# The last ten result tiles of a convolution-and-MLP kernel, stored one by one instead of in pairs

## Chip, cores, metric

One core of a Trainium2 chip. The metric is device microseconds of one execution. The kernel before takes 695.6 us (median of 3 runs, 695.6 to 696.04).

## The reference, cut to what matters

```python
# attention part: causal convolution, 7 taps, softmaxed per-head weights, x is (8, 4096, 192)
out = np.einsum('hk,bskhg->bshg', w, x_unf)
# then, on the 32768 rows:
h = x @ w_in                 # 192 -> 2048
g = np.maximum(0.01 * h, h)
return (g @ w_out)           # 2048 -> 192, float32
```

## The kernel before

The output is 256 tiles ("sums") of 128 rows by 192 columns. TensorE accumulates each in a PSUM bank, an engine copies it to SBUF, and SyncE's queue stores it. Two neighbouring sums share one SBUF buffer and go out in one store of 192 KB:

```python
o_pool = ctx.enter_context(tc.tile_pool(name="o", bufs=4))
...
NSUB = len(subs)             # 256
LAST = NSUB - 2 * SUB        # 248: the sums of the last block
...
def evac_o(n):
    b, e, s = subs[n]
    rp, st = divmod(b, NB)
    if n % 2 == 0:
        osb[n // 2] = o_pool.tile([128, 2, D], FP32, name="o_sb")
    o_sb = osb[n // 2]
    copy = nc.scalar.copy if b < NHALF else nc.vector.tensor_copy
    ins = copy(out=o_sb[:, n % 2, :], in_=po.pop(n))
    if n % 2 == 1:
        t0 = st * ST + (s - 1) * 128
        nc.sync.dma_start(
            out=out_rows[2 * rp + e, t0 : t0 + 256, :].rearrange("(c p) d -> p c d", p=128),
            in_=osb.pop(n // 2),
        )
    return ins
...
evac_o(LAST - 1)
for n in range(LAST, NSUB):            # nothing but these matmuls is left here
    po[n] = psum_o.tile([128, D], FP32, name="po", tag="po")
    for fc in range(NFC):
        mm2_one(None, n, fc, fc == 0, fc == NFC - 1)
    evac_o(n)
```

## Time and profile before

| part of the span | us | what it is |
|---|---|---|
| start to 689.91 | 689.9 | TensorE busy, 99% |
| to 690.31 | 0.4 | VectorE copies the last sum |
| to 692.33 | 2.0 | the last store: issue, packets, confirmation |
| to 692.68 | 0.35 | closing waits of SyncE, after the landing |
| to 693.5 | 0.8 | drains and barrier of all engines |

The span in the trace is 693.5 us; the measured time of that execution is 695.24 us, so 1.7 us lie around it. A store has "landed" when its semaphore, a counter that finished transfers raise, has its full value. The "closing waits" are the end of the program on SyncE: it waits for nine semaphores, one after the other. The rows come from the timeline and from windows cut at its times. The prediction below shows those lines. "The tail" in what follows is the last three rows: from the end of the last copy to the end of the span. Read with the page's rounding it is 693.5 - 690.31 = 3.19 us; the instruction records themselves give 3.235.

The page's list of transfers has the stores as one group, 128 of 192 KB, with the median time from issue to landing as its last column:

```profile
out_dram<-o_sb SPq DMA_DIRECT2D x128, 192.0 KB, 2.1
```

### The profile page before, as it was taken

Reading aid. Unit: us, or ns where it says so; the run is one execution under the profiler, and the core shown is the slowest. Engines: PE = TensorE matmul, PEld = TensorE weight load, DVE = VectorE, ACT = ScalarE, POOL = GpSimd, SP = SyncE. Lnnn points to the kernel's source line nnn. Section 1 sums busy time; section 2 is a strip of 40 time slices with the busy share of each in tenths; the row PEclk is TensorE's granted clock in tenths of the full one; section 3 lists DMA queues with packets and bytes.
Section 4 is the critical chain, followed back from the end, with each engine's and each line's share of the span. In section 5 each row is a group of like instructions: output and inputs, shape, how many; then the busy total and the mean of one; then the engine's idle time right before and its main releaser. Section 6 shows DMA issues by size and latency. Waiting matters only on the chain.

```text
span 693.5 us, 26049 instructions
## 1 busy us (share of the span) xinstructions
PE 683.7 (99%) x11778; PEld 539.4 (78%) x11778; DVE 543.9 (78%) x1005; ACT 516.4 (74%) x577; POOL 139.7 (20%) x195
## 2 busy tenths in 40 slices
PE   7999999999999999999999999999999999999997
PEld 5899998677777777777777777777777777777777
DVE  7899998977878787878787878877878878777812
ACT  6788888977777777777777777777777777777771
POOL 3632201502222202222112222102222022000000
PEclk9999999999999999999999999999999999999999
DMA  9995535935566345565355564545655365222112
GB/s 169 122 103 81 88 66 79 92 75 74 67 93 81 68 82 69 73 87 82 68 80 77 75 82 82 77 67 80 80 82 81 70 82 68 62 60 62 45 36 70
DMA packets 184015, 54.39 MB, mean 78 GB/s; under 512 B 148320, under 2 KB 183136, under 8 KB 183904
## 3 DMA queue, kind: packets, MB, share of 16 engines
q0 software_dynamic: 97936, 14.17, 30.3%
q1 hardware_dynamic: 85968, 38.56, 22.4%
q8 instruction: 92, 1.51, 1.0%
q14 instruction: 19, 0.16, 0.1%
HBM read 29.88 MB, written 25.17 MB: 79 GB/s over the span
## 4 chain that ended last, share of the span: by engine, by line
PE 93%; DMA 3%; DVE 2%; ACT 1%; POOL 0%; issue 0%; SPq 0%; POOLq 0%; DVEq 0%
PE po L391 48%; PE ph L365 45%; DVE yt L180 2%; DMA w_in<-in_moe_w_in_dram 1%; DMA x_nat<-in_x_dram 1%; DMA xt<-x_bf 1%; ACT g L372 0%; POOL sel L226 0%; DVE yt L174 0%; ACT x_bf L126 0%; POOL w_in L236 0%; PE ptr L141 0%; DVE x_bf L126 0%; SPq L441 0%; POOL sel L224 0%
## 5 line engine op out<-in xcount | busy, mean ns | idle before, releaser
L372 ACT ACTIVATE g<-ph 128x1024 bf16<-128x1024 f32 x512 | 496.2, 1021 | 156.2 <-PE ph L365 155.8
L180 DVE SCALAR_TENSOR_TENSOR yt<-xt,wk,yt 128x512 bf16<-128x512 bf16 (+1 forms) x648 | 442.3, 683 | 17.6
L391 PEld LDWEIGHTS <-g 64*128 64x128 bf16 (+1 forms) x8064 | 352.2, 94 | 45.3 <-issue 0.2
L391 PE MATMUL po<-w_out,g 64*128 64x192 bf16 (+1 forms) x8064 | 382.7, 243 | 0.0
L365 PE MATMUL ph<-yt,w_in 64*128 64x512 bf16 (+1 forms) x3552 | 379.3, 347 | 2.7 <-DMA w_in<-in_moe_w_in_dram 1.1
L365 PEld LDWEIGHTS <-w_in 64*128 64x128 bf16 x3552 | 186.5, 94 | 98.1 <-issue 4.6
L77 POOL DMA_DIRECT2D x_bf<-in_x_dram x180 | 133.7, 774 | 422.1 <-DMA xt<-x_bf 419.7
L438 DVE COPY o_sb<-po 128x192 f32<-128x192 f32 x216 | 77.1, 357 | 121.5 <-PE po L391 115.5
L174 DVE TENSOR_SCALAR yt<-xt,wk 128x512 bf16<-128x512 bf16 (+1 forms) x108 | 37.5, 347 | 2.0 <-DMA xt<-x_bf 1.9
L438 ACT COPY o_sb<-po 128x192 f32<-128x192 f32 x40 | 12.8, 320 | 1.9
L248 PE MATMUL warm<-zero 128*128 128x256 bf16 x24 | 4.8, 348 | 1.1 <-DVE junk L216 1.1
L199 PE MATMUL acc<-xt,diag 64*64 64x256 bf16 x84 | 5.2, 270 | 0.5 <-DVE xt L155 0.5
L199 PEld LDWEIGHTS <-diag 64*64 64x64 bf16 x84 | 4.3, 106 | 1.2 <-DVE xt L155 0.8
L303 ACT ACTIVATE diag<-ident,whm 128x64 bf16<-128x64 bf16 x14 | 3.5, 335 | 1.9 <-DVE whm L289 1.9
L248 PEld LDWEIGHTS <-zero 128*128 128x128 bf16 x24 | 2.4, 118 | 2.1 <-DVE junk L216 1.1
L494 POOL COPY pjunk<-g 1x1 bf16<-1x1 bf16 x1 | 0.2, 176 | 16.0 <-ACT g L372 16.0
L126 DVE CAST x_bf<-x_nat 128x384 bf16<-128x384 f32 x5 | 2.3, 454 | 1.4 <-DMA x_nat<-in_x_dram 1.4
L141 PE MATMUL ptr<-ident,x_bf 64*128 64x64 bf16 x48 | 1.4, 191 | 1.8 <-ACT x_bf L126 0.9
L141 PEld LDWEIGHTS <-x_bf 64*128 64x128 bf16 x48 | 1.0, 95 | 2.8 <-ACT x_bf L126 2.2
L236 POOL DMA_DIRECT2D w_in<-in_moe_w_in_dram x4 | 2.6, 660 | 0.0
L155 DVE COPY xt<-ptr 128x384 bf16<-128x384 bf16 x7 | 2.2, 351 | 0.5 <-PE ptr L141 0.4
L253 ACT ACT_TABLE_LOAD x1 | 1.3, 1283 | 0.8 <-PEq L530 0.8
(35 smaller groups left out, 12.9 us busy)
## 6 DMA issues: line engine op xcount, KB each, us to landing
out_dram<-o_sb SPq DMA_DIRECT2D x128, 192.0 KB, 2.1
x_bf<-in_x_dram POOLq DMA_DIRECT2D x180, 64.0 KB, 3.4
x_nat<-in_x_dram SPq DMA_DIRECT2D x8, 192.0 KB, 4.0
w_in<-in_moe_w_in_dram POOLq DMA_DIRECT2D x4, 384.0 KB, 9.7
xt<-x_bf SPq DMA_TRANSPOSE x90, 2.6
w_out<-in_moe_w_out_dram POOLq DMA_DIRECT2D x1, 768.0 KB, 16.3
w<-in_weight_dram SPq DMA_DIRECT2D x1, 0.2 KB
```

The source lines that it names most:

```text
L77: nc.gpsimd.dma_start(out=t[:, c, :, e, :], in_=src[2 * rp + e, :, :, c * CH : (c + 1) * CH],)
L141: nc.tensor.transpose(out=ts[i][:, s, c, :], in_=x_bf[q // 2][ps, c, (q % 2) * HS + s, :, :].rearrange("p e k -> p (e k)"), identity=ident ...
L174: lambda s=src, d=dst, c=c: nc.vector.tensor_scalar_mul(d, s, wk[:, c, 0:1])
L180: lambda s=src, d=dst, c=c, k=k: nc.vector.scalar_tensor_tensor(out=d, in0=s, scalar=wk[:, c, k : k + 1], in1=d, op0=mybir.AluOpType.mult, ...
L199: lambda k=k, p=p, a=a, e=e, ps=ps: nc.tensor.matmul(out=acc[ps, :T], lhsT=diag[c][ps, p, k, :], rhs=xt[0][ps, c, a : a + T], start=(k == ...
L236: nc.gpsimd.dma_start(out=w_in[e * CH : (e + 1) * CH, :, fs], in_=moe_w_in[:, fs].rearrange("(c p) f -> p c f", p=CH),)
L248: nc.tensor.matmul(out=wa[:, 0, 0:HT], lhsT=zero[:, 0:128], rhs=zero, start=True, stop=True)
L303: nc.scalar.activation(out=diag[c][:, 1, k, :], in_=ident2, func=mybir.ActivationFunctionType.Copy, scale=whm[:, c, 1, k : k + 1],)
L365: nc.tensor.matmul(out=ph[:, e, i * T : (i + 1) * T], lhsT=w_in[ps, c, f * 128 : (f + 1) * 128], rhs=y[ps, c, t0 : t0 + T], start=(c == 0) ...
L372: act = nc.scalar.activation(out=g[blk][:, nf * u : nf * (u + 1), :, t0 : t0 + T], in_=ph.rearrange("p e (i t) -> p i e t", i=nf), func=my ...
L391: return nc.tensor.matmul(out=po[m], lhsT=g[b][ps, fc, e, s * 128 : (s + 1) * 128], rhs=w_out[ps, fc, :], start=start, stop=stop,)
L438: ins = copy(out=o_sb[:, n % 2, :], in_=po.pop(n))
```

## The change

The intent is that the end of the program should not wait for a 192 KB store of which half was ready earlier. From sum 246 on, each sum has its own buffer and its own store of 96 KB.

```diff
     LAST = NSUB - 2 * SUB
+    SINGLE = LAST - 2
...
-        if n % 2 == 0:
+        if n % 2 == 0 or n >= SINGLE:
             osb[n // 2] = o_pool.tile([128, 2, D], FP32, name="o_sb")
...
-        if n % 2 == 1:
+        if n >= SINGLE:
+            t0 = st * ST + s * 128
+            nc.sync.dma_start(
+                out=out_rows[2 * rp + e, t0 : t0 + 128, :], in_=osb.pop(n // 2)[:, n % 2, :]
+            )
+        elif n % 2 == 1:
```

## The prediction

> **What bounds the kernel now.** I read the page's first two parts, then the chain of work that ended last, then the timeline, the waits and the transfer windows of the last 16 us only, since the change touches nothing earlier.
>
> ```profile
> span 693.5 us, 26049 instructions
> PE 683.7 (99%) x11778; PEld 539.4 (78%) x11778; DVE 543.9 (78%) x1005; ACT 516.4 (74%) x577; POOL 139.7 (20%) x195
> ...
> PE 93%; DMA 3%; DVE 2%; ACT 1%; POOL 0%; issue 0%; SPq 0%; POOLq 0%; DVEq 0%
> ```
>
> TensorE is busy 99% of the span at full clock, and 93% of the chain is matmuls. Stores do not appear in that chain's shares at all (the 3% DMA are loads at the start). So over 690 us the stores run beside matmuls, and a store can matter only after the last matmul. The timeline of the end says how much time that is (columns: start us, length us, engine, line, operation, tiles, count, idle before):
>
> ```profile
> 677.75 12.16 PE L391 MATMUL po<-w_out,g 64*128 64x192 bf16 x160
> ...
> 687.31 0.36 DVE L438 COPY o_sb<-po 128x192 f32<-128x192 f32 x1 [0.96 <-PE po L391]
> 688.63 0.36 DVE L438 COPY o_sb<-po 128x192 f32<-128x192 f32 x1 [0.96 <-PE po L391]
> 689.95 0.36 DVE L438 COPY o_sb<-po 128x192 f32<-128x192 f32 x1 [0.96 <-PE po L391]
> ```
>
> The last matmuls end at about 689.9. The eight sums of the last block come out one every 1.32 us, VectorE copies each in 0.36 and then idles 0.96 waiting for the next. The last copy ends at 690.31, so 3.2 us of the span have no compute in them. The answer for the store line shows its issue on the SyncE queue and its landing:
>
> ```profile
> L441 SPq DMA_DIRECT2D out_dram<-o_sb x128: 372/372/536, 31.7 to 690.3; - x128
> ...
> DMA to landing us min/median/max: 2.0/2.1/4.6
> ```
>
> The last store starts its issue at 690.33, needs 0.372 us on the queue whatever it waits for, and lands about 2.0 us after the start, at 692.33. I cut the end into windows at those times (the columns end with clock, DMA busy share and GB/s):
>
> ```profile
> 690.71:691.20 0.49, 0.00 (x0) 0.00 (x0) 0.00 (x0) 0.00 (x0) 0.00 (x0) 1.00 0.00 0
> 691.20:691.90 0.70, 0.00 (x0) 0.00 (x0) 0.00 (x0) 0.00 (x0) 0.00 (x0) 1.00 0.81 279
> 691.90:692.33 0.43, 0.00 (x0) 0.00 (x0) 0.00 (x0) 0.00 (x0) 0.00 (x0) 1.00 0.01 4
> 692.33:692.68 0.35, 0.00 (x0) 0.00 (x0) 0.00 (x0) 0.00 (x0) 0.00 (x0) 1.00 0.00 0
> 692.68:693.50 0.82, 0.00 (x0) 0.00 (x0) 0.00 (x0) 0.00 (x0) 0.00 (x0) 1.00 0.00 0
> ```
>
> So the tail is: issue 0.38, nothing moving 0.49, packets 0.70, nothing moving until the store counts as landed 0.43, then 0.35 and 0.82 of closing. The 0.35 has its own row. The end of the program (L541) on the SyncE queue, in 692.28 to 692.70, then in 690.70 to 692.00:
>
> ```profile
> L541 SPq EVENT_SEMAPHORE  x6: 28/28/28, 692.3 to 692.6; - x6
> ```
>
> ```profile
> L541 SPq EVENT_SEMAPHORE  x3: 27/28/28, 690.8 to 690.9; - x3
> ```
>
> Nine closing waits in one order: three pass at once, the fourth holds for 1.4 us (the table of waits gives that figure, on the store), and with the fourth's release five more follow, about 0.06 us apart (six starts between 692.3 and 692.6).
>
> **What the Trainium skill says.** "DMA: Bandwidth & Descriptors", section "Anatomy of one DMA", splits a transfer into a fixed part of about 2.0 us, mostly confirmation of the last write, and bytes at 436 GB/s. It describes the GpSimd path; this store, from SyncE, takes 2.0 us for 192 KB in all, so the fixed part here is smaller, about 1.4 us (2.0 less the 0.6 computed below). The split itself fits: 0.70 us has packets and the rest none. "Perfetto Trace Analysis", the table for the hardware-generated DMA instruction (its T5 to T8), says that the profiled instruction ends before the data moves and that the semaphore write follows confirmation of the data; the trace agrees, with packets 0.5 us after the issue ends and a landing 0.43 us after they end. The first page's "Rules for kernel authors" says to coalesce small transfers, below 64 KB being mostly overhead. That speaks against this change in general; a single sum is 128 x 192 x 4 bytes = 96 KB, still above it.
>
> **The change part by part.** Sums 246 to 255 now each take their own buffer and are stored when copied: five 192 KB stores become ten of 96 KB. Building both kernels and comparing the order shows no other movement: TensorE, ScalarE and GpSimd have the same instructions in the same order, SyncE five more stores, and every VectorE copy of the ten a wait for an old store (before, only every second copy had it).
>
> Part one, the early halves. Sums 246, 248, 250, 252 and 254 leave up to 1.32 us earlier. All are landed before the end either way, so 0 us.
>
> Part two, the last store's size. Sum 255 ends the program. Its matmuls and its copy are unchanged, so its issue still starts at about 690.33. It has half the bytes. During the dense part of a store the engines show 326 GB/s (the half microsecond 691.3 to 691.8), so 196,608 bytes take 0.60 us and 98,304 take 0.30: 0.30 us saved. Row length stays 192 x 4 = 768 bytes, so the rate should not fall. I leave issue (0.37), start (0.49) and confirmation (0.43) as they are: fixed parts. Sum 254's store is issued 1.32 us before and its packets, 0.9 to 1.25 us after its issue starts, are through by about 690.3, well before 255's start at 691.2.
>
> Part three, the closing waits. The built programs wait at the end for eight hardware-queue semaphores in the fixed order 0 to 7, after one other wait. Stores take these semaphores in turn. Before, the last store used number 2: it is the fourth wait, which is just what the trace shows (three passed, the fourth held). Five more stores move the last one to number 7, the ninth and last wait. The other eight then pass while 255 is still moving: from about 690.75 at 0.06 us each they are done by 691.2, and 254 has landed by about 689.0 + 1.7 = 690.7. So the five waits after the landing, 5 x 0.058 = 0.29 us, leave the end.
>
> Part four, costs. Five more issues of 0.372 us on SyncE: the queue has 1.32 us per sum, so they fit, 0 us. Ten buffers taken instead of five from a pool of four: the copy of sum n waits for the store of n-4, issued 4 x 1.32 = 5.3 us before and landed 2 us later, so about 3 us to spare, 0 us. The added wait on each copy: copies that already had it start 1.32 us after one another just like those without (687.31, 688.63, 689.95), so 0 us.
>
> Sum: -0.30 - 0.29 = -0.59 us, from 695.6 to 695.0.
>
> **The rivals.** First, the transfer is all fixed cost: halving the bytes saves nothing, because the first-packet delay and confirmation rule. For it speaks that 1.4 of 2.0 us do not depend on the packets; against it, that packets fill 0.70 us without a gap and the landing follows their end. Only the closing waits would remain: 695.3.
>
> Second, the closing waits are not worth their 0.29 us, because the final barrier of the other engines sets the end. The trace speaks against it: the other engines' closing entries start only at 692.8 or later, behind SyncE's. Then the time would be 695.3 as well, and with both rivals 695.6.
>
> Third, the smaller buffers bite: with four buffers used twice as fast, a store that lands late holds a copy, and the last copy slips. The longest landing in the kernel is 4.6 us, still under 5.3, and the last 10 us have no other traffic of note. It would cost up to a microsecond: 696.5. I hold this unlikely.
>
> Fourth, the big saving that a reader may hope for, half a pair's 2.64 us: the early half of the last pair was never what the end waited for, so it isn't there.
>
> **Range and chances.** The effect is 0.1% of the time; three runs before lie 0.44 us apart, nearly as much as the gain. So the range is 694.5 (a gain of 0.6 with a low draw) to 695.7 (a rival right and nothing gained, with a little noise). A change of 2% would need 14 us, over four times the whole tail after the last copy; on the slow side nothing in the tail can cost that either. Within 2%: 0.98, each side 0.01.
>
> **What would show it.** Right: the last copy still ends at about 690.3; the last store's packets fill about 0.35 us rather than 0.70; it lands about 1.7 us after its issue starts; only one SyncE closing wait is left after that landing, and the closing after it is 0.82 us plus at most 0.1; span near 692.9. Ten single stores of 96 KB would stand in the table of issues, and VectorE's idle before their copies would still be put down to matmuls alone. Wrong: a VectorE idle put down to a store (third rival), the same 2.0 us landing at half the bytes (first), or a span that keeps its length although SyncE is through earlier (second). If the copies of the last sums start later than before, my claim that the added waits are free has failed.

## The result

The changed kernel took 695.2 us (median of 6 runs, 693.82 to 696.42), the kernel before in the same rounds 695.82 (6 runs, 695.5 to 696.48). Ratios here are the mean time of one kernel's runs over that of the other's of the same rounds, so not quite the ratio of these medians. The ratio is 0.9989 with a 95% interval of 0.9977 to 1.0002: same within 2%, and by the times alone not even surely below one. The trace has to say whether the 0.6 us is real.

The page of the changed kernel begins:

```profile
span 693.2 us, 26064 instructions
PE 684.1 (99%) x11778; PEld 539.5 (78%) x11778; DVE 544.4 (79%) x1005; ACT 516.4 (74%) x577; POOL 139.6 (20%) x195
...
out_dram<-o_sb SPq DMA_DIRECT2D x123, 192.0 KB, 2.1
out_dram<-o_sb SPq DMA_DIRECT2D x10, 96.0 KB, 1.6
```

The bound is the same. Ten stores of half the size land in 1.6 us rather than 2.1. The span is only 0.3 us shorter, half of what the tail gives. The timeline says why (start us, length us, engine, line, operation, tiles, count, idle before):

```profile
688.96 0.36 DVE L439 COPY o_sb<-po 128x192 f32<-128x192 f32 x1 [0.96 <-PE po L392]
690.28 0.36 DVE L439 COPY o_sb<-po 128x192 f32<-128x192 f32 x1 [0.96 <-PE po L392]
```

The last copy starts at 690.28, which is 0.33 us later than before. Copies are still 1.32 us apart and VectorE's idle is still put down to matmuls, so the end part did not cause this. Comparing the n-th matmul of both traces finds the delay in two places: 0.07 us at 12.6 us into the run, where TensorE waits for the weights w_in to arrive, and 0.26 us more by 136 us, where it waits once for the convolution. From 180 us on TensorE is busy without a gap in both, and the delay stays 0.33. Nothing in those stretches differs between the two programs. It is the scatter of single runs, measured further below.

The windows of the tail after the change answer to those shown of before (the last two columns are the DMA engines' busy share and GB/s):

```profile
690.64:690.99 0.35, 0.00 (x0) 0.00 (x0) 0.00 (x0) 0.00 (x0) 0.00 (x0) 1.00 0.00 0
690.99:691.47 0.48, 0.00 (x0) 0.00 (x0) 0.00 (x0) 0.00 (x0) 0.00 (x0) 1.00 0.00 0
...
691.47:691.90 0.43, 0.00 (x0) 0.00 (x0) 0.00 (x0) 0.00 (x0) 0.00 (x0) 1.00 0.69 229
...
692.29:692.37 0.08, 0.00 (x0) 0.00 (x0) 0.00 (x0) 0.00 (x0) 0.00 (x0) 1.00 0.00 0
692.37:693.20 0.83, 0.00 (x0) 0.00 (x0) 0.00 (x0) 0.00 (x0) 0.00 (x0) 1.00 0.00 0
```

The reader sees issue, then nothing, then packets for 0.43 us where it was 0.70, confirmation until 692.29, then 0.08 us of closing waits where it was 0.35. (The windows were cut by hand; by the packets' own records it is 0.45 us where it was 0.75.) In the window 692.00 to 692.37 the closing waits of SyncE, six before, are one:

```profile
L547 SPq EVENT_SEMAPHORE  x1: 28/28/28, 692.3 to 692.3; - x1
```

From the records, the wait that holds for the last store passes 2.030 us after the end of the last copy before and 1.673 after: 0.36 us less. From there to the first drain it is 0.369 before and 0.065 after: 0.30 less. From that drain to the end it is 0.836 and 0.841. The tail went from 3.235 to 2.579 us, 0.66 less, and two thirds of a microsecond in 695.8 would be a ratio of 0.9991.

### The profile page after: what moved, and what is told of

It reads as the page before. It is cut to its first block, busy times and chain, and to the rows that moved or that the text cites. A ratio compares the mean times of both kernels' runs of the same rounds, so it can differ in the third digit from the quotient of the medians.

```text
span 693.2 us, 26064 instructions
## 1 busy us (share of the span) xinstructions
PE 684.1 (99%) x11778; PEld 539.5 (78%) x11778; DVE 544.4 (79%) x1005; ACT 516.4 (74%) x577; POOL 139.6 (20%) x195
## 4 chain that ended last, share of the span: by engine, by line
PE 93%; DMA 3%; DVE 2%; ACT 1%; POOL 0%; issue 0%; SPq 0%; POOLq 0%; DVEq 0%
PE po L392 48%; PE ph L366 45%; DVE yt L180 2%; DMA w_in<-in_moe_w_in_dram 1%; DMA x_nat<-in_x_dram 1%; DMA xt<-x_bf 1%; ACT g L373 0%; POOL sel L226 0%; DVE yt L174 0%; ACT x_bf L126 0%; POOL w_in L236 0%; PE ptr L141 0%; DVE x_bf L126 0%; SPq L447 0%; POOL sel L224 0%
```

## The experiments

Edits are shown against the changed kernel unless it says otherwise, cut to what matters. My theory had two terms: the size of the very last store, and the number of closing waits that stand behind it. The rivals were that the size does it alone, that the wait order does it alone, that the early leaving of all ten sums matters, and that the 0.6 us was chance. Eight hardware-queue semaphores are used by turns and waited for in fixed order at the end, so adding a store anywhere moves the last store's place among the closing waits. That makes both terms separately adjustable.

**Only the last two sums singly.**

```diff
-    SINGLE = LAST - 2
+    SINGLE = NSUB - 2
```

> Only sums 254 and 255 are stored singly; eight others of the ten go back to pairs. The measure is the tail, from the end of the last VectorE copy to the end of the span: 3.19 us in the kernel before, 2.56 with ten singles. The built program puts the last store on semaphore 3, the fifth of the nine closing waits, so four follow its landing. My theory (last store's size, plus closing waits after it, 0.057 us each): landing about 1.65 us after the issue starts, tail 2.56 + 4 x 0.057 = 2.79. Rival 'size alone': 2.56 to 2.6. Rival 'it takes all ten leaving early': near 3.1. Whole time: the differences are below what the runs scatter by, so same.

Measured: the last store's wait passes after 1.671 us as with ten, then four more follow it, and the tail is 2.83 us (theory 2.79). The row of closing waits in the window 692.00 to 692.50 has the wait that held and its four followers:

```profile
L547 SPq EVENT_SEMAPHORE  x5: 28/28/28, 692.1 to 692.4; - x5
```

Size alone falls, and so does the claim that all ten must leave early: the whole saving in landing time is here already with two. Time 695.41 us against 696.23, ratio 0.9988 (0.9975 to 1.0).

**Ten other sums singly, the last ten in pairs.**

```diff
-    SINGLE = LAST - 2
+    SINGLES = range(LAST - 12, LAST - 2)
...
-        if n % 2 == 0 or n >= SINGLE:
+        if n % 2 == 0 or n in SINGLES:
...
-        if n >= SINGLE:                 # the single store
+        if n in SINGLES:
```

> Sums 236 to 245 are stored singly and the last ten in pairs again, so the last store is 192 KB as before, but the number of stores is that of the changed kernel and the last one sits on semaphore 7, the last closing wait. My theory: landing 2.0 us as before, no wait after it, tail 3.19 - 5 x 0.057 = 2.9. Rival 'size alone': 3.19. Rival 'the wait order alone': 2.56 to 2.6. Whole time: same.

Measured: 192 KB again, passing after 2.041 us; one closing wait; tail 2.94 us (theory 2.9). Here are the packets of the last store, and the piece from its landing to the first drain:

```profile
690.83:691.56 0.73, 0.00 (x0) 0.00 (x0) 0.00 (x0) 0.00 (x0) 0.00 (x0) 1.00 0.82 268
...
691.95:692.02 0.07, 0.00 (x0) 0.00 (x0) 0.00 (x0) 0.00 (x0) 0.00 (x0) 1.00 0.00 0
```

The long packets of before stand beside the short closing of after. A store's place in the list is worth 0.30 us although nothing at the end was made smaller or earlier. Time 695.77 us against 696.23, ratio 0.9992 (0.998 to 1.0005).

**Twelve sums singly.**

```diff
-    SINGLE = LAST - 2
+    SINGLE = LAST - 4
```

> Twelve sums singly rather than ten: one store more, and with it the last one moves to semaphore 0, the second of the nine waits, with seven after its landing. My theory: landing 1.65 us as with ten, tail 2.56 + 7 x 0.057 = 2.96, that is 0.4 us worse than ten singles although more leave early. Rival 'more singles, or size alone': 2.56 or less. Whole time: same, perhaps 0.4 us above ten singles if the scatter allows to see it.

Measured: going two sums further in the same direction, the tail grows to 3.09 us, nearly that of the kernel before. The theory said 2.96; the wait passed 0.05 us later than with ten (1.723), the rest is waits slightly over 0.06 us each. In 692.80 to 693.46, after the one that held:

```profile
L547 SPq EVENT_SEMAPHORE  x8: 27/28/28, 692.9 to 693.4; - x8
```

Seven waits behind the landing, as foreseen. Time 696.0 us against 696.23, ratio 0.9994 (0.9981 to 1.0008).

**The changed kernel again.** No edit.

> The changed kernel unaltered, for its scatter and a second trace. My theory: the tail repeats within 0.05 us (2.5 to 2.6), as does the landing of 1.65 us, while the time at which the last copy ends moves by several tenths from run to run. Whole time against before: 0.6 us less, with an interval that this many rounds may or may not free from zero. Rival 'the 0.6 us was chance': tail back near 3.2.

Measured: tail 2.55 us, the wait passes after 1.661, one closing wait. So the tail repeats within 0.03 us, and the rival "chance" falls. The span was 694.0, longer than before's 693.5, for the last copy ended at 691.49, 1.2 us later than before. The table of waits of TensorE, in 80 to 140 us, names the largest cause (total us, times, longest):

```profile
PE ph L366 <- DVE yt L180: 1.2, 1, 1.2
```

One wait for the convolution, early on, is nearly twice the change. Matmul by matmul, 0.34 us were lost before 30 us, 1.14 more by 128 us, and 0.31 made up again by 153 us. Over the traces so far the last copy ended anywhere from 689.91 to 691.49. Time 695.69 us against 696.23, ratio 0.9990 (0.9978 to 1.0003).

**All 256 sums singly.**

```diff
-    SINGLE = LAST - 2
+    SINGLE = 0
```

> All 256 sums are stored singly, 128 stores more than before. The last one sits on semaphore 2 as before (128 is a multiple of eight). My theory: tail 2.56 + 5 x 0.06 = 2.86 us, so worse than ten singles by 0.3; no stall in the middle, because a sum comes every 2.6 us there and four buffers give 10.4 us, against a transpose burst of about 4.5 us on the SyncE queue and a landing of 1.65 us. Whole time same as before within 2%. Rival 'more stores cost everywhere' (each 0.33 us on SyncE, smaller transfers): VectorE or ScalarE copies wait for stores, TensorE idles, time up by several us.

Measured: tail 2.87 us, wait passing after 1.664 with five behind it. In 692.96 to 693.35 they stand with the one that held:

```profile
L547 SPq EVENT_SEMAPHORE  x6: 27/28/28, 693.0 to 693.3; - x6
```

One copy in the whole run, at 141.7 us, waited 1.9 us for a store, which happens in neither trace of the change nor in that of before; so my "no stall in the middle" missed one, but TensorE did not wait for it anywhere. Time 695.69 us against 695.59, ratio 0.9998 (0.9981 to 1.0014). This run also completes a square, in which both terms are changed each with and without the other:

| tail, us | last store is 4th of nine waits | last store is 9th |
|---|---|---|
| last store 192 KB | 3.24 (before) | 2.94 (ten other sums) |
| last store 96 KB | 2.87 (all singly) | 2.58 (the change) |

Down a column the size is worth 0.37 and 0.36 us, along a row the place 0.30 and 0.29. The two simply add. Each number is of one trace, except that the change has a second (2.55), so differences of 0.03 us mean nothing here.

**Last two sums singly, and eight earlier ones.** The number of stores and the last one's place are those of the change, but sums 246 to 253 go in pairs.

```diff
-    SINGLE = LAST - 2
+    SINGLES = (*range(LAST - 12, LAST - 4), NSUB - 2, NSUB - 1)
...                                     # the rest as with ten other sums
```

> Sums 254 and 255 singly, 246 to 253 in pairs again, and sums 236 to 243 singly in their place, so that the number of stores and the last one's semaphore (7, the last closing wait) are those of the changed kernel. My theory: tail 2.56, as with ten, because only the last store's size and its place among the closing waits count. Rival 'eight others leaving early is worth something': tail above 2.56, by the share of the gain that is theirs.

Measured: tail 2.58 us, as with ten (2.579 here and in the first trace of the change). Eight of the ten sums of the change gain nothing by leaving earlier; they serve only as four of the five added stores that move the last one back in the list of waits.

**One buffer for the ten single sums.**

```diff
+    o1_pool = ctx.enter_context(tc.tile_pool(name="o1", bufs=1))
...
+            pool = o1_pool if n >= SINGLE else o_pool
+            osb[n // 2] = pool.tile([128, 2, D], FP32, name="o_sb")
```

> The ten single sums share one buffer of their own instead of a pool of four. My theory of what the four buffers are worth: each copy now waits for the store before it, 0.36 copy + 0.03 + 1.63 landing + 0.04 = about 2.06 us apart instead of 1.32, so the last copy starts 9 x 2.06 = 18.5 us after the first of the ten instead of 10.7: the span grows by about 7.8 us, with the VectorE's idle put down to the stores; the tail after the last copy stays 2.56. Rival 'the buffers do not matter here, TensorE sets the pace': span unchanged.

Measured: span 703.2 us (one look, 704.88 us), 10.0 more than the change instead of the 7.8 expected, and a tail of 2.57. The timeline of VectorE shows the new wait:

```profile
685.69 0.36 DVE L441 COPY o_sb<-po 128x192 f32<-128x192 f32 x1 [1.76 <-DMA out_dram<-o_sb]
689.63 0.36 DVE L441 COPY o_sb<-po 128x192 f32<-128x192 f32 x1 [3.58 <-DMA out_dram<-o_sb]
691.76 0.36 DVE L441 COPY o_sb<-po 128x192 f32<-128x192 f32 x1 [1.77 <-DMA out_dram<-o_sb]
```

Copies are 2.12 us apart rather than 2.06 (9 x 0.06 = 0.5 us), and one store took 3.4 us to land, which adds 1.8. The changed kernel has such a late store too (2.9 us, where the others take 1.6 to 1.8), and there nobody waits. So the pool of four does real work, and its margin was judged rightly: it covers 5.3 us.

The traces also show what stands beside the late store. With one buffer, 120 of its 128 packets are through by 687.34, and the last eight start only from 688.40 on. In between, from 687.17 to 688.41, one packet of 16 KB is under way on the queue that the profile calls "instruction". The transfers of 686.90 to 688.30 list it (packets, MB, share of the engines):

```profile
q8 instruction: 1, 0.02, 5.6%
```

All twelve traces have such a store, issued between 684.7 and 686.2, with a sixteenth of its packets held back and one such packet beside it; the ten whose landing is recorded took 2.9 to 3.9 us. So it is no rare accident. That the 16 KB packet causes it fits all of them, but no run removes that packet.

**Going on: the last sum in two stores.** First by partitions, 64 and 64, the place kept at the ninth wait.

```diff
-    SINGLE = LAST - 2
+    SINGLE = LAST
...
+            parts = [(0, 64), (64, 128)] if n == NSUB - 1 else [(0, 128)]
+            for lo, hi in parts:             # one store of rows lo to hi each
```

> Going on in the same direction: the last eight sums singly, and sum 255 in two stores of 64 partitions (48 KB) one after the other on the SyncE queue; the last one is on semaphore 7 again. My theory: the second issue starts one issue (0.33 + 0.05) later, and its packets take half of 0.44, so tail 2.56 + 0.38 - 0.22 = 2.72: worse than ten singles. Rival 'half the bytes always saves': 2.56 - 0.22 = 2.34.

Measured: tail 3.51 us, worse than the kernel before, and 0.8 worse than I expected. The row of these stores on the queue has most of the reason in its third figure, the longest issue, which belongs to the two halves (0.550 and 0.578 us):

```profile
L445 SPq DMA_DIRECT2D out_dram<-o_sb x9: 332/333/578, 681.3 to 691.2; - x9
```

A store of 64 partitions takes longer to issue than one of 128 with twice the bytes. Against the expectation the second issue started 0.22 us later and took 0.25 longer, its packets began 0.16 later after it, and they took 0.37 us instead of 0.22, which is 0.15 more: 0.78 in all. (From the first packet to the last, both stores take 1.0 us, but 0.28 of that is a gap between the two.) So another split, by columns, was to tell apart "64 partitions" from "two stores back to back":

```diff
# against the split before
-    parts = [(0, 64), (64, 128)] ...         # rows
+    parts = [(0, 96), (96, 192)] ...         # columns
```

> As the experiment with two 64-partition stores for sum 255, but split by columns: two stores of all 128 partitions with 96 columns (384 bytes a row). It tells whether the 0.55 us issues and the 1.0 us of packets there came from having 64 partitions or from having two stores back to back. If from the 64 partitions: issues of 0.33 us again and a tail of 2.56 + 0.38 - 0.22 = 2.72, some tenths more if 384-byte rows move slower. If from two stores back to back: tail near 3.5 again. Either way worse than ten singles.

Measured: issues of 0.333 and 0.424 us and a tail of 2.93. So it was the 64 partitions that made the first issue 0.55 us, not the pair of stores; coming second costs only some 0.09 us. The tail is 0.2 over the 2.72 expected. The windows of the packets show two bursts with a gap:

```profile
691.46:691.76 0.30, 0.00 (x0) 0.00 (x0) 0.00 (x0) 0.00 (x0) 0.00 (x0) 1.00 0.60 163
691.76:691.93 0.17, 0.00 (x0) 0.00 (x0) 0.00 (x0) 0.00 (x0) 0.00 (x0) 1.00 0.00 0
691.93:692.25 0.32, 0.00 (x0) 0.00 (x0) 0.00 (x0) 0.00 (x0) 0.00 (x0) 1.00 0.60 154
```

The second issue is 0.09 us longer than expected and the second burst 0.10 longer (0.32 instead of 0.22): that is the 0.2. The Trainium skill, "DMA: Bandwidth & Descriptors", section "Specifications", gives 512 bytes as the least transfer for full rate. Whether the rows of 384 bytes cost anything for that reason is not shown: from 96 to 192 KB with rows of 768 bytes the packets took 0.30 us more (0.45 to 0.75), and at that pace 48 KB would take an estimated 0.45 - 0.15 = 0.30 us, hardly less than the 0.30 and 0.32 measured. My "half of 0.44" took no account of the part that does not shrink with the bytes. Why 64 partitions issue slowly is not settled by these runs. Either way, both splits tried lose to one store per sum.

**The last copy on ScalarE.** The one piece left on the path that another idle engine does faster.

```diff
-        copy = nc.scalar.copy if b < NHALF else nc.vector.tensor_copy
+        copy = nc.scalar.copy if b < NHALF or n == NSUB - 1 else nc.vector.tensor_copy
```

> Ten singles as in the changed kernel, but the very last sum is copied by the idle ScalarE (320 ns for such a copy earlier in the kernel) rather than VectorE (357 ns). My theory: the part from the end of the last copy on stays 2.56 us, and the part between the last matmul and the end of that copy shrinks from 0.395 to about 0.36 us. A gain of 0.04 us, which the whole time can't show. Rival: the extra waits that ScalarE takes on (eight stores' semaphores it never waited for) sit ahead of the copy and cost more than 0.04.

Measured: the last matmul ends at 690.11 and the copy, in the timeline, at 690.47, so 0.36 us as expected against 0.395; tail 2.57.

```profile
690.15 0.32 ACT L439 COPY o_sb<-po 128x192 f32<-128x192 f32 x1 [10.70 <-PE po L392]
```

From last matmul to end it is 2.93 us, against 2.97 and 2.95 in the two traces of the change and 3.63 before: the shortest end of all kernels here, by little. Time 694.86 us against 695.6, ratio 0.9987 (0.9973 to 1.0). From last matmul to the copied sum it beats the change by 0.04 us; by the times it can't be told from the change.

## Why the prediction was right

The time (695.0 said, 695.2 measured) and the range were right, but with single runs scattered by more than the gain that is the lesser proof. The range, 694.5 to 695.7, reached up to a gain of nothing, so lying in it could not tell my theory from its rivals; and the kernel before itself took 695.82 us in these rounds rather than the 695.6 I started from. What counts is the tail: 0.59 us less predicted, 0.66 measured. The steps:

- *Early halves, 0 us.* Right: the run with eight of the ten in pairs again has the same tail, 2.58 us. (Sum 254 can't be tested apart from 255.)
- *Last store's size, 0.30 us.* Right in kind, short in size: 0.36. The packets went from 0.75 to 0.45 us, the predicted 0.30. (The 0.70 for packets and 0.43 for confirmation in my text come from a window cut too early; the records give 0.75 and 0.37.) The mis-sized term is the issue, which I held fixed: it is 0.332 us instead of 0.372, and the pause before the first packet is 0.015 shorter. Confirmation did stay, 0.367 and 0.368 us.
- *Closing waits, 0.29 us.* Right: 0.30, and the square shows it with either size of store. My working had the first eight waits done by 691.2; in fact they pause for 0.37 us after the third and the eighth comes at 691.83. The store lands at 692.3, so it cost nothing. What the pause is, no run tells.
- *Five more issues, buffers, an added wait on copies: 0 us.* Right: copies stay 1.32 us apart, and none waits for a store. One buffer shows what it would be without the margin. But "no other traffic of note" in the last 10 us was wrong: the 16 KB packet described above stands beside a store of 2.9 us in the change, which the margin covers.
- *The sign that the last copy would end near 690.3.* Wrong as a sign: it ended at 690.64, and 691.49 in the repeat; the span was 693.2 and 694.0 instead of 692.9. The idle time that moves it lies in the first 180 us, and I should have named the tail, not a time from the start, as the thing to check.
- *The rivals.* "All fixed cost" and "closing waits worth nothing" each fall by a column or row of the square. "Buffers bite" needs a pool of one.

The expected whole-time effect can't be called shown by times: the two runs of the change give 0.9989 and 0.9990, beside the 0.9991 that the tail would make, but both intervals reach past one.

## What to carry to other kernels

In this kernel only the last store counts after the last matmul, so that one is worth making small; but both splits of it below one sum lost again (tails of 2.93 and 3.51 us against 2.58). Look at what the program waits for after its last store, and in which order: a store more or less anywhere can move the last one to the front or the back of that list. And when a gain is smaller than the scatter of whole runs, measure the stretch it is in, from an event that the change can't move.

## What the Trainium skill lacked or had wrong

- "DMA: Bandwidth & Descriptors", section "Anatomy of one DMA": the fixed cost of about 2.0 us is for the GpSimd path; for stores from SyncE's queue the page has a first-byte latency of about 0.6 us but no such split. Here 192 KB took 2.0 us and 96 KB 1.6 us in all, of which all but the packets (0.75 and 0.45 us) is about 1.2 us; the first packet came 0.83 to 0.89 us after the start of the issue, and about 0.50 after its end.
- The same page has no issue times by shape for such stores: 0.372 us for 128x2x192, 0.332 for 128x192 (0.345 where only the last two sums were single), 0.333 and 0.424 for 128x96, but 0.550 and 0.578 for 64x192.
- No page has the closing waits of a program as a cost: about 0.06 us each behind the last landing, up to 7 of them here, 0.3 us between the change and the kernel before.
- No page has a store with a sixteenth of its packets held back while a 16 KB packet of the instruction queue is under way: 2.9 us in the changed kernel and 3.4 with one buffer, among others of mostly 1.6 to 1.8.
